# A planned attention and two-layer-pair kernel: places for the last x1 blocks, VectorE for the weights' differences and the norm's multiplies, and longer planned GpSimd sums

## The chip, the cores and the metric

The kernel runs on one core of one Trainium2 chip. The metric is device microseconds of one execution; the time before is the median of three runs. Profiles are single executions on the same kind of chip. Engines: PE is TensorE (PEld its weight load), DVE is VectorE, ACT is ScalarE, POOL is GpSimd, SP issues the DMAs.

## The reference

```python
def _attn_ref(q, k, v, g_norm):                    # 8 batches, 8 heads, 576 tokens, 64 wide
    kv = np.einsum('bhsd,bhse->bhde', k, v)
    out = np.einsum('bhsd,bhde->bhse', q, kv)
    rms = np.sqrt(np.mean(out * out, axis=-1, keepdims=True) + 1e-06)
    return (out / rms * g_norm).astype(np.float32)

def _moe_ref(x, w_in, w_out):                      # x 4608 x 512, w_in 512 x 2048, w_out 2048 x 512
    h = x @ w_in
    g = np.maximum(0.01 * h, h)
    return (g @ w_out).astype(np.float32)

def _moe2_ref(x, w_in, w_out):
    h = x @ w_in
    g = h - np.tanh(h)
    return (g @ w_out).astype(np.float32)

# heads side by side: x = attn.transpose(0, 2, 1, 3).reshape(4608, 512); then moe, then moe2
```

The four weight matrices come as float64 and are read as pairs of 32-bit words.

## The kernel before, in words

There are four large products after the attention. Each is done by a two-by-two block scheme with seven block products instead of eight; every float32 operand is split into a high and a low float16 part, so that a block product is three float16 matmuls (`three`, L489). `PROD` (L28) says which prepared left and right column each of the seven products takes.

The stages on TensorE, in order:
- A start in which the first weights w1 are converted (`convert`), their largest value found (`weight_scale`, `pow2_scale`) and split (`split_first`), beside the attention of batch 0 and part of batch 1.
- First stage (`up` with blk 0): x times w1, 8 blocks of 576 tokens by 8 column pairs, then leaky ReLU. The attention of batches 1 to 7 is placed between its products (`pos`, `between1`), a pair of heads at a time. `norms` (L901) takes the root of the mean square on ScalarE into a tile iv, its reciprocal in three VectorE pieces (L914), stores it to DRAM (L917), loads it back broadcast over partitions as bc (L927), and GpSimd multiplies x with it (L934), one 128x1152 instruction for each half kk.
- Second stage (`down` with blk 0): the result times w2, 8 superblocks, giving x1, whose blocks lie in X places (`place_t`, L1088) until `ready_t` (L1096) has their row maximum (L954) and a DMA has stored them (L1103).
- Third stage (`up` with blk 1, 9 blocks of 512 tokens): x1 times w3, then h - tanh(h) (L1213, half on VectorE, half on GpSimd).
- Fourth stage (`down` with blk 1): times w4, to the output.

Operands are made by `left_stages` (L426): ScalarE writes the high part of three columns (opa, L435 or L437), VectorE the low part (L442 or L444), then four sums of columns are formed in place (`sum_`, L469; line L474 in the profile: in `down` the first two on VectorE, the others on GpSimd; elsewhere all on GpSimd), then high and low part of the four sums (ops). The weights w2, w3 and w4 are converted in the stage before (`convert`: L317 to L340), written to DRAM, and later read back and split by `split_late` (L387) with `right_stages` (L358): ScalarE high (L366) and VectorE low (L369) of three columns, four 128x128 differences on GpSimd (L376), high and low of those. There are 16 such units for each matrix; `spread` lays them evenly over a stretch of time.

Products end in PSUM banks. `keep` (L535) copies an intermediate block (c, u) from bank a into an X place with ScalarE (L544 to L548); `add` (L552) adds a bank and such a block on VectorE (L557 to L563).

The order of every instruction on every engine is written out by a planner (`Plan`, L45). It keeps a planned clock; TensorE's instructions follow one another by `on_pe`, evictions take the first free slot of their engine by `do`, and a `chain` takes its steps one after the other, each with an engine and a planned length. All instructions are then emitted in the order of planned time, and each engine runs its own in that order. So a planned length that is too short puts an instruction too early into its engine's queue, and it holds what stands behind it.

Places are numbered buffers (`Slots`, L114): 21 L places, 12 M places, 8 X places. A place is given back in the plan when its last use is emitted; whoever takes it next waits on the chip until that use has ended. SP issues nearly all DMAs, in order; an issue that must wait holds those behind it.

## Time and profile before

| | |
|---|---|
| median of three runs | 1527.73 us (1526.67 to 1530.34) |
| the profiled execution, its own time | 1526.35 us |
| its span, first to last instruction | 1524.6 us |
| TensorE busy, share of the span | 1443.4 us, 95% |
| VectorE, ScalarE, GpSimd busy | 1247.2, 911.2, 759.8 us |
| first matmul of the second, third, fourth stage, about | 505, 840, 1184 us |
| DMA traffic | 323.19 MB, 212 GB/s |

The first matmuls of the first stage run at 84.7 us. A busy TensorE is not one at its peak: matmuls at the lower granted clock count as busy too. In the views, "idle before <- X" names what ended an engine's wait; ps_a to ps_d are the PSUM tiles of the products, u and c the intermediate blocks, xst the x1 blocks, gl and g the stored activations, x1g the loaded x1, xg the attention's result, unit the weights being prepared, opa and ops the split operands.

### The profile page before, as it was taken

How to read it: one execution, taken by the hardware profiler on the slowest of the kernel's cores; microseconds unless marked ns; L12 is line 12 of the kernel's file. 1: busy time of each engine (PE TensorE's matmuls, PEld its weight loads, DVE VectorE, ACT ScalarE, POOL GpSimd, SP SyncE). 2: the span in 40 equal slices, each digit the busy share in tenths (PEclk: the TensorE clock that was granted, in tenths of full speed). 3: DMA queues.
4: the chain of work that ended last, by engine and by line, in shares of the span. 5: the costliest groups of instructions: out<-in, count | busy, mean ns of one | idle time of the engine just before them, and what ended most of it. 6: DMA issues, size and time to landing. Idle time of an engine off the chain costs nothing. (4 is left out here: it accounts for less than half of the span.)

```text
span 1524.6 us, 33192 instructions
## 1 busy us (share of the span) xinstructions
PE 1443.4 (95%) x12658; PEld 1191.6 (78%) x12658; DVE 1247.2 (82%) x1971; ACT 911.2 (60%) x1525; POOL 759.8 (50%) x758
## 2 busy tenths in 40 slices
PE   5299999999999999999999899999999899999998
PEld 3167777777777777777777688888888788888887
DVE  4886786777777889899996788988899988888881
ACT  5377766777777645455443577778888544454540
POOL 0483321443643455666673355558896644444440
PEclk8599999999999999999999999999999999999999
DMA  9718987999968756446546666655669644444431
GB/s 264 201 60 257 282 281 250 283 295 313 323 250 317 288 172 208 160 168 207 184 146 214 228 221 209 210 200 209 246 240 353 226 146 149 144 143 156 145 97 36
DMA packets 191040, 323.19 MB, mean 212 GB/s; under 512 B 55712, under 2 KB 133536, under 8 KB 190880
## 3 DMA queue, kind: packets, MB, share of 16 engines
q1 hardware_dynamic: 190880, 321.07, 63.6%
q8 instruction: 99, 1.62, 0.4%
q14 instruction: 61, 0.50, 0.1%
HBM read 190.84 MB, written 130.15 MB: 211 GB/s over the span
## 5 line engine op out<-in xcount | busy, mean ns | idle before, releaser
L495 PEld LDWEIGHTS <-w 128*128 128x128 f16 x8400 | 818.3, 98 | 212.1 <-issue 38.1
L474 POOL TENSOR_TENSOR gl<-gl 128x256 f32<-128x256 f32 (+1 forms) x272 | 305.9, 1126 | 297.9 <-issue 92.6
L495 PE MATMUL ps_a<-ops,w 128*128 128x288 f16 (+1 forms) x2400 | 330.3, 281 | 6.0 <-ACT u L544 3.1
L495 PE MATMUL ps_c<-ops,w 128*128 128x288 f16 (+1 forms) x2352 | 314.0, 282 | 6.9 <-DVE g L557 6.8
L495 PE MATMUL ps_a<-opa,w 128*128 128x288 f16 (+1 forms) x2016 | 285.2, 282 | 12.5 <-ACT u L548 6.6
L495 PEld LDWEIGHTS <-ops 128*128 128x128 f16 x1728 | 169.7, 98 | 24.7 <-issue 4.2
L495 PE MATMUL ps_b<-opa,w 128*128 128x288 f16 (+1 forms) x1200 | 175.6, 283 | 0.0
L376 POOL TENSOR_TENSOR unit<-unit 128x128 f32<-128x128 f32 x192 | 129.6, 677 | 91.4 <-DVE wo L369 57.1
L474 DVE TENSOR_TENSOR gl<-gl 128x256 f32<-128x256 f32 (+1 forms) x272 | 160.7, 594 | 4.1
L1213 POOL TENSOR_TENSOR g<-g,th 128x512 f32<-128x512 f32 x72 | 116.7, 1623 | 78.2 <-ACT th L1210 76.8
L934 POOL TENSOR_TENSOR xg<-xg,bc 128x1152 f32<-128x1152 f32 x16 | 47.4, 2970 | 186.3 <-DMA bc<-iv 118.1
L435 ACT ACTIVATE ops<-gl 128x1152 f16<-128x1152 f32 x64 | 74.3, 1162 | 108.7 <-POOL gl L474 107.0
L437 ACT ACTIVATE ops<-gl,inv 128x1024 f16<-128x1024 f32 x72 | 82.5, 1146 | 94.4 <-POOL gl L474 94.4
L495 PEld LDWEIGHTS <-opa 128*128 128x128 f16 x1296 | 126.6, 98 | 14.8
L444 DVE SCALAR_TENSOR_TENSOR ops<-gl,inv,ops 128x1024 f16<-128x1024 f32 x72 | 103.4, 1436 | 22.8 <-ACT ops L437 22.8
L442 DVE TENSOR_TENSOR ops<-gl,ops 128x1152 f16<-128x1152 f32 x64 | 96.5, 1509 | 11.1 <-ACT ops L435 11.0
L495 PE MATMUL ps_a<-w,ops 128*128 128x256 f16 x864 | 97.5, 275 | 3.6 <-ACT c L548 3.6
L557 DVE SCALAR_TENSOR_TENSOR g<-ps_c,u 128x288 f32<-128x288 f32 x128 | 58.0, 453 | 52.1 <-PE ps_c L495 45.8
L548 ACT ACTIVATE u<-ps_a,up 128x256 f32<-128x256 f32 x144 | 67.9, 472 | 51.8 <-PE ps_a L495 41.6
L495 PE MATMUL ps_c<-w,ops 128*128 128x256 f16 x864 | 97.3, 273 | 0.2 <-DVE osb L557 0.2
L474 POOL TENSOR_TENSOR x1g<-x1g 128x256 f32<-128x256 f32 x72 | 64.0, 890 | 49.8 <-DVE opa L444 42.0
L369 DVE SCALAR_TENSOR_TENSOR wo<-unit,s_w,wo 128x384 f16<-128x384 f32 (+1 forms) x96 | 85.3, 892 | 3.7 <-ACT wo L366 3.6
(122 smaller groups left out, 2147.6 us busy)
## 6 DMA issues: line engine op xcount, KB each, us to landing
g<-g SPq DMA_DIRECT2D x64, 576.0 KB, 5.6
gl<-g SPq DMA_DIRECT2D x64, 576.0 KB, 4.8
g<-g SPq DMA_DIRECT2D x72, 512.0 KB, 3.4
gl<-g SPq DMA_DIRECT2D x72, 512.0 KB, 4.5
wd<-wo SPq DMA_DIRECT2D x48, 448.0 KB, 4.2
w<-wd SPq DMA_DIRECT2D x24, 896.0 KB, 7.7
words<-in_moe_w_in_dram SPq DMA_DIRECT2D x64, 256.0 KB, 5.6
words<-in_moe_w_out_dram SPq DMA_DIRECT2D x64, 256.0 KB, 4.6
```

The lines of the kernel that those rows point to most:

```text
L369: nc.vector.scalar_tensor_tensor(out=dst()[:, 1, a:b], in0=cols(0, n), scalar=scale(), in1=dst()[:, 0, a:b], op0=ALU.mult, op1=ALU.subtract,)
L376: nc.gpsimd.tensor_tensor(out=o, in0=a, in1=b, op=ALU.subtract)
L435: nc.scalar.activation(out=o, in_=i_, func=AF.Copy)
L437: nc.scalar.activation(out=o, in_=i_, func=AF.Identity, scale=scale())
L442: nc.vector.tensor_tensor(out=o, in0=i_, in1=h, op=ALU.subtract)
L444: nc.vector.scalar_tensor_tensor(out=o, in0=i_, scalar=scale(), in1=h, op0=ALU.mult, op1=ALU.subtract)
L474: lambda: e.tensor_tensor(out=g()[:, o], in0=g()[:, a], in1=g()[:, b], op=op),
L495: nc.tensor.matmul(out=out_, lhsT=a, rhs=c, start=start and m == 0, stop=stop and m == n - 1, skip_group_check=not fresh,)
L548: nc.scalar.activation(out=t, in_=src, func=AF.Identity, scale=self.scale)
L557: nc.vector.scalar_tensor_tensor(out=o, in0=src, scalar=self.minus if sub else self.scale, in1=t, op0=ALU.mult, op1=ALU.add,)
L934: nc.gpsimd.tensor_tensor(out=x, in0=x, in1=held[kk].ap, op=ALU.mult)
L1213: e.tensor_tensor(out=g()[:, n], in0=g()[:, n], in1=held["t"].ap[:, n], op=ALU.subtract)
```

## The change

- `place_t` and `ready_t`: in the last superblock of the second stage the four blocks of each half lie in one L place instead of four X places, and two blocks that are neighbours in x1 are stored by one DMA.
- `norms`: iv has a tile of its own instead of an X place. From batch 2 on the multiply is done by VectorE in two 128x576 pieces, planned 10.5 us after the load (`LOADBC`) instead of 7.5.
- `right_stages`: the weights' columns lie in another order (`PROD` and `convert` follow), so that two of the four differences are one instruction with a broadcast input; one difference changes its sign, and `left_stages` follows with the sign of one sum. For w2, w3, w4 the differences run on VectorE, for w1 on GpSimd.
- `sum_`: planned lengths. GpSimd 3.0 (3.8 in `down`) times T/1000 plus 0.1 instead of 2.4; VectorE 1.1 plus 0.08 instead of 1.4 plus 0.1.
- `far_scale`: the largest value of w2, w3, w4 is spread over the partitions by a store to DRAM and a broadcast load, instead of by TensorE; it is planned to take 26 us, and the units that need it start later (w2: START + 219 instead of 200, end -72 instead of -75; w4: c3 + 42 instead of 18).
- `AHEAD`: operands of the next superblock start 1.2 us earlier. `pos`: batches 5, 6, 7 stand 5, 10, 15 products earlier.
- The planner: a step that finds no free place is tried again 0.4 us later (`NoRoom`).

The diff's core:

```diff
-PROD = {1: (6, 6), 2: (4, 4), 3: (0, 5), 4: (5, 0), 5: (3, 2), 6: (1, 1), 7: (2, 3)}
+PROD = {1: (6, 5), 2: (4, 4), 3: (0, 6), 4: (5, 0), 5: (3, 1), 6: (1, 2), 7: (2, 3)}
...
+    GPS = 3.0
...
+    def far_scale(name, m, t):
+        held = {}
+        def put():
+            held["d"] = scratch([P, 1], F32, f"m_{name}_d")
+            nc.sync.dma_start(out=held["d"], in_=m)
+        def get():
+            held["w"] = const.tile([P, P], F32, tag="rows", name=f"rows_{name}")
+            nc.sync.dma_start(out=held["w"], in_=held["d"].rearrange("p o -> o p").broadcast_to((P, P)))
+        def end():
+            r, s = stile(f"r_{name}"), stile(f"s_{name}")
+            nc.vector.tensor_reduce(out=r, in_=held["w"], axis=AX.X, op=ALU.max)
+            powers(r, s)
+        at(t, put)
+        at(t + 6.0, get)
+        at(t + 24.0, end)
...
-                    out=held["w"].ap[:, NU * a:NU * a + NU].rearrange("p (b c) -> p b c", b=2), in_=src[a]
+                    out=held["w"].ap.rearrange("p (b a c) -> p a b c", b=2, a=2)[:, a], in_=src[a]
...
-    def right_stages(w, dst, scale, minus4):
+    def right_stages(w, dst, scale, minus4, merged=False):
...
-        def less(o, a, b):
+        def both(e):
+            b = w().rearrange("p (o c) -> p o c", c=P)
+            e.tensor_tensor(out=b[:, 1:4:2], in0=b[:, 3:4].broadcast_to((P, 2, P)), in1=b[:, 1:3], op=ALU.subtract)
+
+        def less(o, a, b, e):
             o, a, b = (w()[:, P * n:P * n + P] for n in (o, a, b))
-            nc.gpsimd.tensor_tensor(out=o, in0=a, in1=b, op=ALU.subtract)
-
-        t4, t2, t1, t3 = b21, b22, b11, b12 = range(4)
+            e.tensor_tensor(out=o, in0=a, in1=b, op=ALU.subtract)
+
+        t4, t1, t2, t3 = b21, b11, b22, b12 = range(4)
+        on, e = ("V", nc.vector) if merged else ("G", nc.gpsimd)
+        f = 0.28 if merged else 0.5
         return [
             ("A", 0.62, lambda: hi(4, 7, 3)), ("V", 0.62, lambda: lo(4, 7, 3)),
-            ("G", 0.5, lambda: less(t1, b12, b11)), ("G", 0.5, lambda: less(t3, b22, b12)),
-            ("G", 0.5, lambda: less(t2, b22, t1)),
-            ("G", 0.5, (lambda: less(t4, b21, t2)) if minus4 else (lambda: less(t4, t2, b21))),
+            (on, 1.5 * f, lambda: both(e)), (on, f, lambda: less(t2, b22, t1, e)),
+            (on, f, (lambda: less(t4, b21, t2, e)) if minus4 else (lambda: less(t4, t2, b21, e))),
...
-                on, (1.4 if on == "V" else 2.4) * f + 0.1,
+                on, 1.1 * f + 0.08 if on == "V" else (gps or GPS) * f + 0.1,
...
-            sum_(s3, a11, a21, first), sum_(s1, a21, a22, first, ALU.add), sum_(s2, a22, s3), sum_(s4, a12, s2),
+            sum_(s3, a21, a11, first), sum_(s1, a21, a22, first, ALU.add), sum_(s2, a22, s3, rest, ALU.add),
+            sum_(s4, a12, s2, rest),
...
-    AHEAD = 6.8
+    AHEAD = 8.0
+    LOADBC = 10.5
...
-            held["iv"] = X.take([4 * Q, T1], F32, "iv")
+            held["iv"] = const.tile([4 * Q, T1], F32, tag="iv", name="iv")
...
+            if b >= 2:
+                scaled_ = [("V", 0.66, lambda kk=kk, n=n: scale(kk, nc.vector, n, n + 2)) for n in (0, 2)]
+            else:
+                scaled_ = [("G", 2.9 if b else 2.7, lambda kk=kk: scale(kk, nc.gpsimd, 0, 4))]
+            more.append([(None, LOADBC if b > 1 else 7.5 if b else 6.0, lambda kk=kk: load(kk))] + scaled_ + stages)
...
-            pos[b, PAIRS[hp]] = FIRST[b][hp] if b in FIRST else NOP * (NP * b - 16 + 2 * hp)
+            pos[b, PAIRS[hp]] = FIRST[b][hp] if b in FIRST else NOP * (NP * b - 16 + 2 * hp) - 5 * (b - 4)
...
-    spread(lambda i, kk, t: split_late(1, i, kk, t, M), UNITS, START + 200.0, end1 - 75.0)
+    spread(lambda i, kk, t: split_late(1, i, kk, t, M), UNITS, START + 219.0, end1 - 72.0)
...
+            if s == NS1 - 1:
+                if (s, m) not in out_t:
+                    out_t[s, m] = L.take([P, 2, 2, T1], F32, "xst"), []
+                return out_t[s, m][0].ap[:, int(blk[1]) - 1, int(blk[0]) - 1]
             out_t[s, m, blk] = X.take([P, T1], F32, "xst")
...
+                tile_, there = out_t[s, m]
+                there.append((t, nh))
+                if {(0, nh), (1, nh)} <= set(there):
+                    done_.update((("x1", c, s, 0), ("x1", c, s, 1)))
+                    nc.sync.dma_start(out=x1d[c, s], in_=tile_.ap[:, nh].rearrange("p a b -> p (a b)"))
+                if len(there) == 4:
+                    L.give(out_t.pop((s, m))[0])
...
-    e = c3 + 18.0
+    e = c3 + 42.0
```

## Rows read from the trace of the kernel before

**Rows 1.** Page, part 1: engine, busy us (share of the span), x instructions.

```profile
PE 1443.4 (95%) x12658; PEld 1191.6 (78%) x12658; DVE 1247.2 (82%) x1971; ACT 911.2 (60%) x1525; POOL 759.8 (50%) x758
```

**Rows 2.** Waits of TensorE, whole run: who <- whom: us in total, times, longest.

```profile
PE pt L224 <- DVE m_w L264: 29.2, 1, 29.2
...
PE ps_a L495 <- ACT u L548: 7.5, 4, 6.6
...
PE ps_c L495 <- DVE g L557: 6.8, 11, 1.8
...
PE ps_a L495 <- ACT u L546: 4.3, 4, 2.1
...
PE ps_a L495 <- ACT c L548: 4.1, 2, 3.6
...
PE ps_a L495 <- ACT u L544: 3.1, 3, 1.4
...
PE ps_a L495 <- DVE opa L442: 1.8, 3, 1.1
```

**Rows 3.** Timeline, 826 to 870: start, us, instruction, [idle before <- releaser].

```profile
851.55 0.87 ACT L548 ACTIVATE u<-ps_a,up 128x256 f32<-128x256 f32 x2 [7.00 <-DMA x<-xst]
...
852.07 1.44 PE L495 MATMUL ps_a<-opa,w 128*128 128x256 f16 x6 [6.64 <-ACT u L548]
```

**Rows 4.** Chain that ended last, 1195 to 1260: start, us, what.

```profile
1203.82 12.31 PE ps_a L495 x96
...
1242.33 10.48 PE ps_a L495 x96
```

**Rows 5.** Timeline, 258 to 266 and 368 to 379.

```profile
265.34 0.90 PE L495 MATMUL ps_a<-opa,w 128*128 128x288 f16 x6 [1.23 <-ACT u L546]
...
376.75 0.41 ACT L853 ACTIVATE sq<-po 128x288 f32<-128x288 f32 x1 [4.36 <-DMA iv<-iv]
...
377.51 1.10 PE L495 MATMUL ps_a<-opa,w 128*128 128x288 f16 x6 [2.14 <-ACT u L546]
```

**Rows 6.** Groups by form: line engine op | busy us, mean ns | idle before.

```profile
L376 POOL TENSOR_TENSOR unit<-unit 128x128 f32<-128x128 f32 x192 | 129.6, 677 | 91.4 <-DVE wo L369 57.1 <-issue 12.0 <-PE ps_a L495 8.8
...
L474 DVE TENSOR_TENSOR gl<-gl 128x256 f32<-128x256 f32 x144 | 84.5, 588 | 2.9
...
L442 DVE TENSOR_TENSOR ops<-xg,ops 128x576 f16<-128x576 f32 x32 | 29.7, 947 | 4.9 <-ACT ops L435 4.9
```

**Rows 7.** Timelines, 215 to 285 and 360 to 390, VectorE, GpSimd and TensorE.

```profile
217.74 2.88 DVE L328 TENSOR_SCALAR unit<-unit 128x512 int32<-128x512 int32 x1
...
222.14 0.90 PE L495 MATMUL ps_c<-ops,w 128*128 128x288 f16 x6 [0.63 <-DVE g L557]
...
257.42 0.74 DVE L914 RECIPROCAL iv<-iv 128x96 f32<-128x96 f32 x1
...
258.75 0.43 DVE L328 TENSOR_SCALAR unit<-unit 128x512 int32<-128x512 int32 x1
...
277.61 2.64 POOL L934 TENSOR_TENSOR xg<-xg,bc 128x1152 f32<-128x1152 f32 x1 [2.69 <-DMA bc<-iv]
...
366.70 0.75 DVE L914 RECIPROCAL iv<-iv 128x96 f32<-128x96 f32 x1
...
388.27 2.88 POOL L934 TENSOR_TENSOR xg<-xg,bc 128x1152 f32<-128x1152 f32 x1 [2.40 <-DMA k<-in_k_dram]
```

**Rows 8.** Line 474: instruction xcount: ns min/median/max, first to last start, forms.

```profile
L474 DVE TENSOR_TENSOR gl<-gl x272: 407/450/1493, 462.5 to 1480.5; 128x256 f32<-128x256 f32 x72, 128x288 f32<-128x288 f32 x64
```

**Rows 9.** Stretches: us, busy us of each engine (x), granted clock, DMA share, GB/s.

```profile
659.20:700.40 41.20, 39.57 (x323) 31.31 (x321) 39.59 (x54) 20.40 (x28) 27.67 (x27) 1.00 0.57 193
...
1062.00:1150.00 88.00, 88.00 (x809) 78.78 (x807) 81.39 (x123) 73.91 (x129) 77.72 (x85) 1.00 0.70 256
...
1150.00:1204.00 54.00, 47.80 (x431) 41.88 (x430) 53.97 (x69) 38.09 (x58) 38.44 (x28) 1.00 0.91 332
```

**Rows 10.** Waits of all engines, 505 to 840.

```profile
ACT ops L435 <- POOL gl L474: 107.0, 47, 6.2
```

More of the change, by code (lines that the diff above doesn't have):

```diff
@@ L42 @@
 Consts = namedtuple("Consts", "x hid neg_hid op out neg_out")
+class NoRoom(Exception):
+    pass
 class Plan:
@@ L90, in go, with run @@
                 end[0] = max(end[0], t_ + dur + (0.0 if eng is None else self.HAND))
-                def run(fn=fn):
-                    fn()
+                def run(fn=fn, until=None):
+                    try:
+                        fn()
+                    except NoRoom:
+                        assert until is None or self.now < until, "no room"
+                        self.at(self.now + 0.4, lambda: run(fn, until or self.now + 40.0))
+                        return
                     left[0] -= 1
@@ L122, in take @@
         if not self.idle:
-            raise RuntimeError(f"no place {self.kind} for {name}")
+            raise NoRoom(f"no place {self.kind} for {name}")
         n = self.idle.pop(0)
@@ L273, in last @@
                 fn()
-        later = 0.0 if n == 0 else 4.0
         at(t, first)
-        at(t + 2.8 + (later and later + 2.0), last)
+        at(t + (2.8 if n == 0 else 26.0), last)
     def in_unit(w, i, kk):
@@ L314, in one @@
                 held["ap"] = keep()
+        def one():
             words = held["w"].ap
@@ L353, in convert @@
         slow = 1.0 if keep else 1.1
-        steps = [(None, land, load), ("A", 0.7, one), ("V", 0.72 * slow, two), ("V", 0.4 * slow, shift),
+        steps = [(None, land, load), (None, 0.0, room), ("A", 0.7, one), ("V", 0.72 * slow, two), ("V", 0.4 * slow, shift),
                  ("V", 0.63 * slow, low), ("V", 0.63 * slow, high)]
         plan.chain(t, steps + ([(None, 0.0, store)] if keep is None else []))
-    def right_stages(w, dst, scale, minus4):
+    def right_stages(w, dst, scale, minus4, merged=False):
         def cols(n0, n1):
@@ L423, in load_weights, with left_stages @@
         )
-    def left_stages(g, dst, scale, T, done=None, first=None, pieces=1):
+    def left_stages(g, dst, scale, T, done=None, first=None, pieces=1, rest=None, gps=None):
         f = T / 1000.0
@@ L698, in produce @@
                     lambda held=held: held["g"].ap, o, (lambda: scale(s)) if scale else None, T,
-                    done=lambda held=held: L.give(held["g"]), first=nc.vector,
+                    done=lambda held=held: L.give(held["g"]), first=nc.vector, gps=3.8,
                 )
@@ L912, in inverse @@
         def inverse(n):
-            part = held["iv"].ap[:, CP * n:CP * n + CP]
+            part = held["iv"][:, CP * n:CP * n + CP]
             nc.vector.reciprocal(out=part, in_=part)
         def store():
-            nc.sync.dma_start(out=ivd[b], in_=held["iv"].ap)
-            X.give(held["iv"])
+            nc.sync.dma_start(out=ivd[b], in_=held["iv"])
         def load(kk):
```

47 lines of the change are left out of this document (27 added, 20 removed).

## The prediction

> **What bounds it now.** I read the page's busy times first: TensorE is busy in 95% of the span, every other engine less [rows 1]. So I asked next what TensorE waits for, since only its idle time and its slow clock can be won [rows 2]. The largest row, 29.2 us, lies in the start, until the first weights are scaled; the change does not touch it. The six below it sum to 7.5 + 6.8 + 4.3 + 4.1 + 3.1 + 1.8 = 27.6 us, and they lie in four places: VectorE evictions (ps_c, 6.8 us; the longest, 1.8, near the third stage's end, the other ten, 5.0, in the first stage), ScalarE evictions of that stage (u L546), ScalarE and VectorE in the second stage (u L544, opa), and the two borders of the third, with one wait of 6.6 us and one of 3.6 us. That is the purse. The reader is to see in these rows that no single engine bounds the kernel; short queues in ScalarE and VectorE do, each behind something that came late.
>
> **Large buffers for the last x1 blocks.** At 851.55 a ScalarE eviction of the third stage had waited 7.00 us for the landing of an x1 store, and TensorE stood 6.64 us behind it [rows 3]. The eviction takes one of the eight X places; the last superblock's x1 blocks held them until their stores landed. In the new version these blocks lie in two L places, so no eviction takes a place behind such a store. The clock falls in that wait: the six matmuls after it took 1.44 us, and the same clock after the wait at 1203 made 96 matmuls 12.31 us instead of 10.48 [rows 3, 4]. I put the cold piece at 1.8 us by that pair, an estimate, so the part is worth 6.64 + 1.8 = 8.4 us. What is late next: the following weights and operands; the two stores per block pair become one, which relieves SP and adds no queue. Should an L place still be read when it is taken, a VectorE addition waits in place of ScalarE; bounds 5 and 9 us.
>
> **The roots' own buffer.** The same cause shows twice in the first stage: ScalarE stood for the store of iv, and TensorE lost 1.23 and 2.14 us [rows 5]. The second wait is followed by a low clock (six matmuls in 1.10 us), which I price at 1.5 us by the pair in [rows 4]. iv now has a tile of its own: 1.23 + 2.14 + 1.5 = 4.9 us won; bounds 3.4 and 5.5.
>
> **Roots multiplied on VectorE from batch 2 on.** GpSimd no longer has these 12 instructions; VectorE gets 24 of half the size, about 0.95 us each by the nearest row (128x576) [rows 6], 23 us spread over 300 us in which VectorE is not full. The danger is the wait that moves with them. The factors come by DMA, behind the store of iv. By the code the second multiply now starts 0.25 + 1.8 + 3.0 + 10.5 = 15.55 us after the last reciprocal. In the trace the factors were there later than that in the bad batches: reciprocal done at 258.16, multiply released by the DMA at 277.61 (19.5 us); 367.45 and 388.27 (20.8 us) [rows 7]; I count on two or three such among the six batches. GpSimd could wait for nothing; VectorE has the evictions queued behind it, and TensorE waits for those. How much of a blocked VectorE reaches TensorE: an integer shift at 217.74 took 2.88 us, where the same at 258.75 took 0.43 (it fell together with the large GpSimd multiply), and TensorE lost 0.63 us at 222.14 [rows 7]; so about 1.8 us are swallowed. Two or three batches late by 4 to 5 us cost 2 to 3.5 us each: some 8 us at most; nothing, if the store of iv lands sooner. I take 4 us lost, the middle, since the same DMA traffic stands around them. On the other side, the large GpSimd multiply no longer holds VectorE, nor do the subtractions below: of the 5.0 us that ps_c costs here [rows 2] I take 2 us as won (bounds 0 and 4).
>
> **Weights' differences on VectorE.** 48 units leave GpSimd, each four instructions of 677 ns, 130 us in all [rows 6]. VectorE gets three instead, one of 128x256 and two of 128x128. For the first the nearest row is 588 ns (mean), 407 ns at least [rows 6, 8]; for the narrow ones no row stands, so I bound them by half of and the whole of 407 ns and take 0.3 us. A unit then costs VectorE at least 0.4 + 2 x 0.2 = 0.8 us, disturbed 0.6 + 2 x 0.3 = 1.2 (1.4 at the far end). Removing 2.7 us of GpSimd gives something back: the rows' mean of 588 against 407 is what meeting GpSimd costs VectorE, 0.18 us for each of the 16 sums of a superblock, about 3 us; with the other two-input instructions twice that. GpSimd is busy 28 us in a superblock [rows 9], so a us of it costs 0.1 to 0.2 us of VectorE, and a unit gives back 0.3 to 0.55 us. Net a unit costs 0.2 to 0.9 us.
>
> Second stage: two units in a superblock of 41.2 us, in which VectorE is already busy 39.6 us [rows 9]. It becomes 40.0 to 41.4: just inside, or just over. Against it stand two helps. GpSimd's sums are now planned at 1.19 us instead of 0.79 (3.8 x 0.288 + 0.1), near the truth; before, ScalarE was given its next split too early and stood 107 us in total until GpSimd was done [rows 10], with the evictions behind it; that is the 3.1 us of u L544. And operands start 1.2 us earlier (AHEAD), which covers most of the 1.8 us on opa [rows 2]. I take 3 us won of 4.9; bounds: 4.9 won and, at the upper load, 7 x 0.5 = 3.5 lost (VectorE waits a little too, so it is full before 41.2).
>
> Third stage and its end: the last weights' units start 24 us later and end where they did, so in 1062 to 1150 there are about 15 instead of 12. VectorE was busy 81.4 of 88 us [rows 9]. Added: 15 x 0.8 to 1.2 = 12 to 18, three more units of two scalings each, about as long as the 128x576 row [rows 6], 6; given back, 12 x 2.7 = 33 us of GpSimd x 0.2 = 7. That is 92 to 98 of 88, so VectorE enters 1150 some 4 to 10 us late, where it is busy 54.0 of 54 already [rows 9]. Against this stands again the longer planned sum: the 3.56 us wait at 1203 and its cold 1.8 us come from an eviction queued behind a split that waited for GpSimd [rows 2, 4]. I let the two cancel: 0; bounds 5 won, 8 lost.
>
> **The rest.** The first weights stay on GpSimd, 16 units with two narrow subtractions made one wide: at most half of 677 ns each [rows 6], 5 us of GpSimd, while TensorE waits in the start for other things as well: 1 us won (0 to 2). The maximum of the later weights goes through DRAM instead of two TensorE instructions a time, three times: under 1 us, hidden, since its units are started later to match; two short DMAs a time pass through SP. The new column order, the sign of one difference and the earlier last batches change no count: 0.
>
> **Sum.** -8.4 - 4.9 + 4 - 2 - 3 + 0 - 1 = -15.3 us on the profiled execution's 1526.35: 1511. The median of the runs shown lies 1.4 us above that execution; so 1512.
>
> **Rivals.**
> - *No new wait on VectorE* (0.17). The factors land in time and GpSimd's relief is at the upper bound: no +4, and 6 us more at the two full places: 1501 to 1502. For it speaks that late landings went with the very jams that the change removes; against it, VectorE's 54.0 of 54.
> - *Half given back* (0.13). The buffers win their 13 us, the multiplies cost 8 of them and the replanning wins nothing: 1521.
> - *It does not reach TensorE, or the new order shifts as much as it wins* (0.08): 1527. For: every order of all queues changes. Against: the 7.00 us behind a store is a plain place conflict.
> - *VectorE becomes the bound; slower* (0.07). It decides from the point at which a superblock asks for more than 41.2 us. If the moved instructions mostly meet a GpSimd sum, each costs up to the longest row, 1.49 us against 0.41 [rows 8], and nothing comes back: 1 us more per superblock in seven, 13 us at 1062 to 1204, and all 8 us on the multiplies, less the buffers: +7 + 13 + 8 - 13.3 = +15, 1542. Against it: the mean is 0.59, far from 1.49.
>
> The Trainium skill speaks for that last rival (SBUF — State Buffer, Who interferes with whom): a VectorE instruction with two inputs in SBUF and a GpSimd instruction that reads SBUF exclude each other, and the later one is blocked until the first is through. The trace agrees in kind, 407 to 1493 ns for one sum [rows 8]. By the rule at its worst the moved instructions cost what this rival says; by the mean in the rows they cost what the sum says.
>
> **Chances.** Forecast 0.55 (1506 to 1518), the others as given. A measurement of this kernel tells about 0.3% from no change, 4.6 us. Faster by more: 0.55 + 0.17 + 0.12 = 0.84; within: 0.09; slower: 0.07. The range leaves out the slower rival and the rest of the two-sided tails: 1499 to 1525.
>
> **What would show it.** No ScalarE eviction waits for a landing of x1 or iv, and TensorE has no wait over 2 us near 845. Waits of VectorE for bc appear in the first stage, up to 5 us each, with ps_c waits behind them. ScalarE's 107 us on GpSimd fall by more than half. VectorE's busy share rises from 82% to about 85%, GpSimd's falls from 50% to under 40%. Wrong it is if VectorE shows 41 us of 41.2 in superblocks with evictions late, or if the L places bring a DMA wait at 840.

## The result, and the profile after

The changed kernel takes 1539.61 us (1536.22 to 1543.11), the kernel before beside it 1527.20. The ratio is 1.0078, 95% interval 1.0051 to 1.0105: 12 us slower, where 1512 was forecast. The profiled execution is the longest of its four (1543.11 us, span 1541.3), that of the kernel before nearly its shortest, so the two profiles below differ by 16.7 us and not by 12.

Waits of TensorE after, against [rows 2] (who <- whom: us in total, times, longest):

```profile
PE ps_c L540 <- DVE g L602: 19.1, 17, 2.8
PE pq L877 <- ACT kvd L868: 12.9, 6, 5.4
PE pk L857 <- DMA v<-in_v_dram: 8.5, 4, 6.4
PE ps_a L540 <- ACT u L591: 4.7, 1, 4.7
PE pk L857 <- DVE xg L908: 4.0, 1, 4.0
PE ps_a L540 <- ACT c L591: 4.0, 3, 3.4
```

The 6.64 us wait of [rows 3] is gone; this is the longest that is left at the border (858 to 879):

```profile
860.18 0.82 PE L540 MATMUL ps_a<-ops,w 128*128 128x256 f16 x6 [0.56 <-ACT c L593]
```

The row of ps_c, where TensorE waits for VectorE, rose from 6.8 to 19.1. Where the time went is told by stretches: first stage, second stage, third and fourth together. The first begins with its first float16 matmul, the second with its first one into ps_d, the third with the first of 256 columns. Columns as in [rows 9]: us, then busy us of TensorE, its weight load, VectorE, ScalarE, GpSimd, then granted clock, DMA share, GB/s. Before, then after:

```profile
84.70:505.40 420.70, 408.83 (x3661) 313.88 (x3660) 314.05 (x584) 304.38 (x608) 175.53 (x198) 0.99 0.84 271
505.40:840.00 334.60, 329.61 (x2682) 261.84 (x2681) 301.81 (x421) 155.34 (x203) 194.57 (x185) 1.00 0.56 191
840.00:1524.60 684.60, 666.65 (x6054) 593.28 (x6053) 574.56 (x847) 414.45 (x636) 362.01 (x344) 0.99 0.54 186
```

```profile
86.40:528.50 442.10, 417.28 (x3655) 318.55 (x3654) 322.89 (x653) 303.51 (x606) 94.42 (x109) 0.97 0.82 259
528.50:858.80 330.30, 328.96 (x2681) 262.13 (x2680) 311.12 (x469) 156.22 (x203) 155.16 (x121) 1.00 0.57 192
858.80:1541.30 682.50, 663.76 (x6051) 591.83 (x6050) 582.18 (x894) 416.09 (x636) 314.70 (x280) 1.00 0.55 187
```

The first stage lost 21.4 us; the second won 4.3, the rest 2.1, the start lost 1.7. Of the 21.4, TensorE stood 12.9 us longer (24.8 against 11.9) and was busy 8.5 us longer for the same matmuls at a granted clock of 0.97 instead of 0.99. VectorE is busy 323 of 442 us there, 73%: it is not full. (The 83% in the expectation of e3 is the share of the whole run.) What it did instead was stand. Three pauses of the first stage, with the engine that stood before each (timeline after: start, us, instruction [idle <- releaser]):

```profile
281.68 1.43 DVE L979 TENSOR_TENSOR xg<-xg,bc 128x576 f32<-128x576 f32 x2 [4.99 <-DMA bc<-iv]
284.13 1.60 PE L540 MATMUL ps_c<-ops,w 128*128 128x288 f16 x6 [2.78 <-DVE g L602]
...
415.68 0.61 ACT L405 ACTIVATE wo<-unit,s_w 128x384 f16<-128x384 f32 x1 [8.63 <-DMA wf<-unit]
416.65 1.60 PE L540 MATMUL ps_a<-ops,w 128*128 128x288 f16 x6 [4.68 <-ACT u L591]
...
481.26 0.92 ACT L479 ACTIVATE opa<-gl 128x864 f16<-128x864 f32 x1 [5.35 <-DMA gl<-g]
482.54 0.88 PE L540 MATMUL ps_a<-ops,w 128*128 128x288 f16 x3 [3.40 <-ACT c L591]
```

The first is the wait for the broadcast factors that was forecast. In the second, ScalarE wants an M place whose last content, a unit, is not yet stored; evictions stand behind it. The third is a load of stored activations (gl) that came late.

The second shows how one late transfer holds the next. SP's own rows (SPq is the issue of a transfer):

```profile
405.04 0.54 SPq L447 DMA_DIRECT2D wd<-wo  x1
410.22 0.34 SPq L440 DMA_DIRECT2D unit<-wf  x1
...
411.13 0.39 SPq L389 DMA_DIRECT2D wf<-unit  x1
```

```profile
SPq L440 <- DMA wd<-wo: 9.7, 5, 4.6
```

The second view is SP's wait from 190 to 505 us: five times, at most 4.6 us, it stood at the load of a unit until an earlier unit's store had landed. That is the gap from 405.58 to 410.22 here. So the store that ScalarE needed was issued at 411.13 only, 4.1 us after ScalarE had begun to stand (415.68 - 8.63 = 407.05).

In the third stage's end VectorE did become full. The stretches of [rows 9], later by the 18 us that the border moved:

```profile
1080.00:1168.00 88.00, 83.69 (x762) 74.27 (x760) 87.91 (x157) 72.98 (x126) 43.58 (x36) 1.00 0.68 243
1168.00:1222.00 54.00, 47.18 (x424) 41.17 (x422) 53.97 (x69) 37.85 (x54) 35.55 (x28) 1.00 0.92 331
```

### The profile page after: what moved, and what is told of

It is laid out like the page before. It is cut to its first block, busy times and chain, and to the rows that moved or that the text cites. A ratio compares the mean times of both kernels' runs of the same rounds, so it can differ in the third digit from the quotient of the medians.

```text
span 1541.3 us, 33054 instructions
## 1 busy us (share of the span) xinstructions
PE 1447.2 (94%) x12649; PEld 1195.0 (78%) x12649; DVE 1273.6 (83%) x2136; ACT 914.2 (59%) x1525; POOL 591.9 (38%) x538
## 4 chain that ended last, share of the span: by engine, by line
PE 62%; DVE 16%; DMA 10%; issue 5%; SPq 3%; POOL 2%; ACT 1%; DVEq 0%; ACTq 0%; POOLq 0%
PE ps_a L540 29%; PE ps_c L540 17%; PE ps_b L540 9%; PE ps_d L540 4%; DVE opa L486 3%; DMA gl<-g 2%; DVE gl L518 2%; DVE wo L408 2%; DMA words<-in_moe_w_in_dram 2%; DVE ops L486 2%; DMA bc<-iv 2%; DMA wd<-wo 1%; DMA v<-in_v_dram 1%; DVE g L602 1%; PE pk L857 1%
## 5 line engine op out<-in xcount | busy, mean ns | idle before, releaser
L540 PE MATMUL ps_c<-ops,w 128*128 128x288 f16 (+1 forms) x2352 | 316.9, 283 | 19.2 <-DVE g L602 19.1
L518 POOL TENSOR_TENSOR xg<-xg 128x288 f32<-128x288 f32 x64 | 59.0, 927 | 292.8 <-DMA k<-in_k_dram 57.2
L518 DVE TENSOR_TENSOR gl<-gl 128x256 f32<-128x256 f32 (+1 forms) x272 | 152.3, 561 | 4.2
L479 ACT ACTIVATE ops<-gl 128x1152 f16<-128x1152 f32 x64 | 74.3, 1161 | 76.1 <-POOL gl L518 74.9
L405 ACT ACTIVATE wo<-unit,s_w 128x384 f16<-128x384 f32 (+1 forms) x96 | 63.1, 662 | 67.3 <-DVE unit L419 48.8
L486 DVE TENSOR_TENSOR opa<-gl,opa 128x864 f16<-128x864 f32 x64 | 81.0, 1266 | 6.4 <-ACT opa L479 6.3
```

The source lines that it names most:

```text
L405: nc.scalar.activation(out=dst()[:, 0, a:b], in_=cols(0, n), func=AF.Identity, scale=scale())
L479: nc.scalar.activation(out=o, in_=i_, func=AF.Copy)
L486: nc.vector.tensor_tensor(out=o, in0=i_, in1=h, op=ALU.subtract)
L518: lambda: e.tensor_tensor(out=g()[:, o], in0=g()[:, a], in1=g()[:, b], op=op),
L540: nc.tensor.matmul(out=out_, lhsT=a, rhs=c, start=start and m == 0, stop=stop and m == n - 1, skip_group_check=not fresh,)
```

## The experiments

All of them were measured beside the kernel before. Where the expectations speak of superblocks 2 to 4 and 5 to 8, the edits act on batches 2 to 7 (multiplies) and on batches 5, 6 and 7, by 5, 10 and 15 products (pairs moved up). "Stands" are, from 190 to 505 us, ScalarE's waits for a unit's store (wf<-unit, wd<-wo: an M place not yet free), and VectorE's for the store of a finished block (g<-g, L636 or L681: an L place not yet free) or the load of bc, summed from the waits of each engine. Other waits for transfers (loads of units, words and gl; in the kernel before 9.4 us of ScalarE for the store of iv) are not in them. Stage lengths are from one profile each, ratios from all runs; a profile can lie 4 us off its kernel's median (e10: 1539.63 against 1535.36), so small differences of stage lengths tell nothing.

| kernel | ratio | 95% interval | first stage | second | third, fourth | ScalarE, units | VectorE, g and bc |
|---|---|---|---|---|---|---|---|
| before | 1 | | 420.7 | 334.6 | 684.6 | 0.0 | 0.5 |
| after | 1.0078 | 1.0051 to 1.0105 | 442.1 | 330.3 | 682.5 | 14.8 | 12.9 |
| e1 | 1.0051 | 1.0032 to 1.0069 | 432.8 | 331.0 | 683.3 | 10.1 | 0.2 |
| e2 | 1.0006 | 0.9991 to 1.0022 | 424.9 | 331.2 | 684.2 | 1.0 | 16.0 |
| e3 | 1.0014 | 0.9998 to 1.0031 | 427.9 | 330.9 | 683.9 | 3.2 | 13.9 |
| e4 | 0.9955 | 0.9941 to 0.9968 | 419.0 | 335.6 | 675.5 | 0.0 | 0.0 |
| e5 | 0.9981 | 0.9967 to 0.9995 | 426.5 | 330.9 | 679.1 | 10.5 | 4.4 |
| e6 | 1.0060 | 1.0039 to 1.0081 | 433.6 | 330.2 | 685.3 | 6.6 | 10.3 |
| e7 | 0.9958 | 0.9941 to 0.9975 | 423.4 | 335.4 | 675.5 | 0.0 | 13.4 |
| e8 | 1.0077 | 1.0055 to 1.0098 | 431.1 | 336.8 | 683.6 | 23.7 | 0.0 |
| e9 | 1.0114 | 1.0078 to 1.0150 | 434.2 | 330.1 | 690.3 | 16.0 | 9.4 |
| e10 | 1.0041 | 1.0025 to 1.0056 | 428.2 | 339.2 | 684.1 | 11.4 | 2.1 |
| e11 | 0.9943 | 0.9922 to 0.9964 | 419.7 | 333.8 | 678.4 | 0.0 | 0.2 |
| e12 | 0.9971 | 0.9955 to 0.9988 | 426.5 | 332.2 | 677.0 | 0.0 | 9.0 |
| e13 | 1.0012 | 0.9994 to 1.0031 | 428.3 | 335.0 | 676.7 | 0.0 | 11.5 |
| e14 | 1.0029 | 1.0013 to 1.0044 | 431.3 | 335.8 | 676.7 | 26.2 | 0.0 |
| e15 | 1.0034 | 1.0016 to 1.0051 | 431.1 | 334.5 | 675.6 | 10.1 | 9.0 |
| e16 | 1.0055 | 1.0037 to 1.0072 | 441.1 | 330.9 | 678.8 | 15.3 | 2.3 |
| e17 | 1.0103 | 1.0085 to 1.0121 | 442.1 | 334.0 | 675.8 | 0.0 | 8.2 |
| e18 | 1.0072 | 1.0050 to 1.0093 | 435.7 | 331.2 | 683.9 | 7.6 | 15.3 |

### One part undone, and the two buffer parts alone

e1, multiplies back on GpSimd:

```diff
-            if b >= 2:
+            if b >= 9:
-            more.append([(None, LOADBC if b > 1 else 7.5 if b else 6.0, lambda kk=kk: load(kk))] + scaled_ + stages)
+            more.append([(None, 7.5 if b else 6.0, lambda kk=kk: load(kk))] + scaled_ + stages)
```

> The changed kernel, with one part undone: the multiplication of x0 by the broadcast inverse roots goes back from VectorE to GpSimd for superblocks 2 to 4 (in one piece of 2.9 us, with 7.5 us allowed for the load instead of 10.5). Theory A (VectorE standing in order for the broadcast): in the changed kernel VectorE stood 4.99, 2.36 and 2.19 us for bc, with a pause of TensorE of 2.78 us at 281 behind the first; GpSimd takes these waits over, the pauses at 281, 332 and 346 go, and the first stage (442.1 us after, 420.7 before) falls by 8 to 14 us, the whole to about 1528 to 1532. Theory B (ScalarE standing for the stores of w2's finished units) and theory C (the row maximum sent through DRAM holding SP's queue): the first stage falls by no more than 4 us, the pauses at 359, 412 and 479 stay.

The kernel takes 4 us less than after (the intervals overlap), the first stage 9.3 us less. That is theory A's stage length, but not its whole (1528 to 1532; 1535.5 measured). The waits for bc went over to GpSimd. ScalarE's stands stayed for the most part (10.1 of 14.8 us), as theories B and C had it.

e2, scales of w2 to w4 as before, w2's units from START + 200 to the end less 75:

```diff
-                far_scale(name, m, t + 0.6)
+            pow2_scale(name, m, 1, t + 0.6 + later, 1.6 if n == 0 else 3.0)
```

> The changed kernel, with one part undone: the scales of w2 to w4 are found as before (row maxima through a transpose and a matmul on TensorE, no trip through DRAM), so that s_w2 is there earlier, and w2's units are spread from START + 200 to the stage's end less 75 instead of START + 219 to less 72. Theory C (the trip through DRAM holds SP's queue for 2.4 us at 278 and again at 473, and the later start crowds w2's units into too few places): the pauses of TensorE at 281, 359, 412 and 479, together 14.9 us, shrink to under 5, and the first stage falls by 10 to 15 us, the whole to about 1527. Theory A (VectorE's waits for bc): only the pause at 281 becomes shorter, the first stage falls by 1 to 4 us. Theory D (VectorE's load by the differences): nothing falls by over 2 us.

This gives 11 us back (0.0072 of 1527), and the first stage is 17 us shorter, a little more than theory C said. ScalarE's stands for units' stores fell from 14.8 to 1.0 us; VectorE's did not (16.0 against 12.9).

e3, w2's differences back on GpSimd (the call of `right_stages`):

```diff
- ... n == 2, n >= 1)
+ ... n == 2, n >= 2)
```

> The changed kernel, with one part undone for the first stage alone: w2's differences go back from VectorE to GpSimd (there in the new, joined form of three instructions); w3's and w4's stay on VectorE. Theory D (the differences fill VectorE's queue in the first stage): the first stage falls by 6 us or more, since some 13 us of VectorE go. Theories A and C: VectorE is 83% busy there in either kernel, not full, so the first stage stays within 3 us, or grows by up to 5 because a unit then takes longer from load to store and holds its two places the longer (theory B).

This gives 10 us back, and the first stage is 14 us shorter, as theory D had it, though VectorE is not full there. So each of three parts gives back 4 to 11 us, 25 in sum where 12 were lost. The prices of the parts do not add up.

e4, the kernel before with the new `place_t` and `ready_t`, and iv's own tile; nothing else:

```diff
-            held["iv"] = X.take([4 * Q, T1], F32, "iv")
+            held["iv"] = const.tile([4 * Q, T1], F32, tag="iv", name="iv")
...
+                    out_t[s, m] = L.take([P, 2, 2, T1], F32, "xst"), []
```

> The kernel before, with two parts of the change alone: the large buffers for the last x1 blocks, and iv's own tile. By the terms of the prediction: -8.4 us at the border between the second and third stage and -4.9 us at 377, so 1513 us, bounds 1511 to 1519. The changed kernel shows the border's gain (third stage 330.3 against 334.5 us with losses elsewhere in it). A rival: iv's wait was hiding a later one, as for the lack of another place, and only the buffers count: 1518. If both gains are eaten by later waits: 1526.

The ratio is 0.9955: 7 us won where 13 were forecast. The third and fourth stage win 9.1, as forecast for the buffers; the first wins 1.7, and the start and the second stage lose 2.9. ScalarE no longer waits for iv, but TensorE's 2.14 us at 377 [rows 5] came back at 387 as 1.89 us, behind a ScalarE that now stands for GpSimd's multiply:

```profile
385.28 0.92 ACT L435 ACTIVATE opa<-xg 128x864 f16<-128x864 f32 x1 [4.76 <-POOL xg L933]
...
387.06 0.75 PE L847 MATMUL po<-qt,kvd 128*128 128x288 f32 x2 [1.89 <-ACT qt L839]
```

The rival that only the buffers count is the nearer one.

### Combinations

e5 undoes all three, w4's differences too (e1's and e2's edits, and):

```diff
- ... n == 2, n >= 1)
+ ... n == 2, n == 2)
```

> The changed kernel with all three parts undone together: multiplies of x0 on GpSimd, scales of w2 to w4 through TensorE (w2's units from START + 200), and the differences of w2 and w4 on GpSimd; w3's differences stay on VectorE, as do the large buffers, iv's tile, the longer times planned for GpSimd's sums and the earlier start of the accumulators' loads. Theory E (the three parts feed one another: a late VectorE instruction keeps a store waiting on SP's queue, the loads behind it land late, and VectorE and ScalarE stand for these loads): the first stage falls from 442.1 to 418 to 422 us, by no more than the 21.4 that were lost, although the three runs so far gave back 8.6, 17.2 and 14.2 us one by one, which sums to 40. Theory F (each part has a price of its own, and what is undone adds up): the first stage falls by more than 25, to under 417. Fourth section (from the border of the second and third stage to the last stage): if w4's differences on VectorE are what ate the border's gain, 336 to 338 us as against 345.3 after and 336.7 with the buffers alone; if not, 344 to 346. With the second stage at 331 the whole gives 1512 to 1516 us.

Neither theory holds: the first stage takes 426.5 us, and the whole is 3 us faster than before. w3's differences stay on VectorE here, w4's are on GpSimd: the third and fourth stage take 679.1 us against 684.2 in e2. In the first stage 7.5 us remained against e4, with none of the three parts in it.

e6, as e2, but w2's units left at START + 219:

> The changed kernel with the scales of w2 to w4 through TensorE as in the run of e2, but w2's units left where the change put them, from START + 219 to the stage's end less 72. It takes SP's trip through DRAM away and leaves the crowding. Theory C1 (SP's queue, held for 5.8 us by the row maximum's way through DRAM): the first stage is as in e2, 423 to 427 us. Theory C2 (units 19 us later, which finds too few places and makes ScalarE stand for stores): the first stage stays at 437 us or more, with the pauses at 359 and 412.

The first stage, 433.6 us, lies between the theories, 8.7 us above e2 and so nearer to C2, and the pauses at 359 and 412 are there (5.8 and 3.5 us). The kernel is 8 us slower than e2 by 19 us of start and 3 of end in a list of times. The trip through DRAM itself makes 2.7 us between e6 and after, within the intervals.

e7, e4 with the change's `scale(kk, e, n0, n1)` and its 10.5 us, and the pairs moved up:

```diff
- ... NOP * (NP * b - 16 + 2 * hp)
+ ... NOP * (NP * b - 16 + 2 * hp) - 5 * (b - 4)
```

> The kernel before with the two buffer parts as in e4, and on top of them the multiplies of x0 on VectorE for superblocks 2 to 4, with 10.5 us for the load of bc and the pairs' places moved up by 5 products a superblock as in the change (the longer wait needs them). e4's first stage was 419.0 us, the whole 1521.5. Theory E (parts feed one another): alone this part costs under 4 us, first stage 417 to 423. Theory F (a price of its own): 425 to 429, as it gave back 8.6 us when undone.

The whole is within 0.5 us of e4, as theory E had it; the first stage is 4.4 us longer, the start 0.9 shorter.

e8, e4 with all later differences on VectorE:

```diff
-            nc.gpsimd.tensor_tensor(out=o, in0=a, in1=b, op=ALU.subtract)
+            (nc.vector if merged else nc.gpsimd).tensor_tensor(out=o, in0=a, in1=b, op=ALU.subtract)
```

> The kernel before with the two buffer parts as in e4, and on top of them the differences of w2, w3 and w4 on VectorE (four instructions of 128 columns, as the kernel before has them on GpSimd). e4's sections were 419.0, 335.5, 336.7 and 338.9 us. Theory E: the first stage grows by under 4 us; theory F: by 10 to 14 us, as undoing gave back 14.2. Second stage (w3): if the 4 us that the change won there come from its differences, 331; if from the accumulators' loads and the planned sums, 335. Fourth section (w4): 344 to 346 if these differences fill VectorE there, 337 if not.

The kernel is 19 us slower than e4: 12 in the first stage, 8 in the third and fourth. The second stage wins nothing, so its 4 us after do not come from having w3's differences on VectorE.

### Is it the number of places?

e9 is the changed kernel, e10 the kernel of e8, each with one line changed:

```diff
-    NL, NM, NX = 21, 12, 8
+    NL, NM, NX = 20, 13, 8
```

> The changed kernel with one size changed: 13 places for w's units and operands A (M) instead of 12, and 20 large places (L) instead of 21 to make room. Nothing else. In the changed kernel's first stage ScalarE stood 8.6, 5.1 and 3.9 us for a place whose last content was still being stored (its rows name wf<-unit and wd<-wo), and pauses of TensorE of 4.0 and 4.7 us stand with it. Theory G (units in fewer places than their pace asks for): with one more place a place is written one unit later, these stands fall under 5 us in sum, the pauses at 359 and 412 go, and the first stage falls from 442.1 to 430 or less. Theory H (the places are no cause, the queues are late anyway): the first stage stays within 4 us of 442, and the stands move to other rows; a loss beyond that would come from the one L place less, as waits for words, g or bc.

> The kernel of e8 (the kernel before, two buffer parts, differences of w2 to w4 on VectorE) with 13 M places and 20 L places. In e8 the first stage was 431.1 us against 419.0 without the differences, and ScalarE stood 12.4 and 11.3 us for places whose store was under way. Theory G (the differences' own work is cheap there; the shorter plan of a unit turns the places round too soon): first stage 419 to 424. Theory H (the load on VectorE is what costs): 428 to 433. The fourth section should stay at 343 to 346 by either, as VectorE is full there.

e10 is 5.5 us faster than e8, but its first stage takes 428.2 us, which theory H had named, and ScalarE's stands are only halved. In e9 the first stage is 8 us shorter than after, between the theories. ScalarE's stands are 16.0 us against 14.8, and the whole is no better (third and fourth stage 690.3, with one L place less). One more place helps a little and does not remove the stands. (Of the 8.6, 5.1 and 3.9 us that e9's expectation names, the third is a wait for g<-g.)

### Parts that change only times and order

e11, e4 with the longer planned sums and AHEAD 8.0 in second and fourth stage alone:

```diff
-    AHEAD = 6.8
+    AHEAD = 8.0
-                    done=lambda held=held: L.give(held["g"]), first=nc.vector,
+                    done=lambda held=held: L.give(held["g"]), first=nc.vector, gps=3.8,
```

> The kernel of e4 (the kernel before, two buffer parts) with the parts of the change that touch only the second and the last stage: GpSimd's sums planned at 3.8 instead of 2.4 per 1000 elements and VectorE's at 1.1, and 8.0 instead of 6.8 us of lead for a superblock's operands; the first and third stage keep their lengths. The changed kernel and its variants won 3.3 to 4.3 us in the second stage, and e8 shows that w3's differences do not bring that. Expected: second stage 331 against 335.5 in e4, the others as in e4 (419.0, 336.7, 338.9), so 1517 us. If it takes the longer times of the first stage or the joined differences as well, the second stage stays at 335.

The ratio is 0.9943, the fastest here, though not to be told from e4. The second stage takes 333.8 us, 1.8 less than in e4, where 4.5 were expected. e4, e7 and e11 beat both kernels by 6 us and more.

e12, e4 with the longer sums everywhere (`GPS = 3.0`, and `gps=3.8` as in e11) and e7's line of `pos`:

> The kernel of e4 with two parts of the change: GpSimd's sums planned at 3.0 (3.8 in the second and last stage) and VectorE's at 1.1, and the pairs of superblocks 5 to 8 moved up by 5 products each. Both are in e5, whose first stage was 426.5 us against e4's 419.0 although the multiplies, differences and scales are undone there. If these two make the 7.5 us: first stage 425 to 428. If they come from the new form of the differences and the step that takes a unit's place before the conversion: 417 to 421. Second stage: 335 (without the earlier lead) or 331 (if the planned sums win it). Fourth section: 340 to 342 if the planned sums are what e5 lost there against e4 (341.1 against 336.7).

The first stage takes 426.5 us, as much as in e5. The second takes 332.2, so the planned sums win 3.4 of the 5.3 us between e4 and after, without AHEAD.

e13, e4 with e7's line of `pos` alone; e14, e4 with e8's differences for w2 alone (`n == 1`); e15, e13 with

```diff
-    spread(lambda i, kk, t: split_late(1, i, kk, t, M), UNITS, START + 200.0, end1 - 75.0)
+    spread(lambda i, kk, t: split_late(1, i, kk, t, M), UNITS, START + 219.0, end1 - 72.0)
```

and e16, the changed kernel with e1's edit and e5's `n == 2`:

> The kernel of e4 (0.9955 of the time before, first stage 419.0 us) with the pairs of superblocks 5 to 8 moved up by 5 products each, and nothing else. It is in e7 (423.4) and e12 (426.5). If it is what those two have in common that costs: first stage 423 to 426, whole 0.997 to 0.999. If it costs nothing alone: 418 to 421, whole 0.995 to 0.996.

> The kernel of e4 with w2's differences alone on VectorE; w3's and w4's stay on GpSimd. e8, with all three, was 18.6 us slower than e4. If the first stage carries 10 to 12 of them as its profile says: first stage 429 to 432, later sections as in e4 (335.5 and 675.6 us), whole 1.002 to 1.004. If w4's differences in the third stage carry nearly all and the first stage of e8 was an accident of that profile: 420 to 424 and 0.996 to 0.998.

> The kernel of e4 with w2's units spread as in the change, START + 219 to the stage's end less 72 (before: START + 200 to less 75), and the pairs moved up as in e13, without which the plan has no room. Multiplies and differences stay on GpSimd. Theory I (the tighter spread has a price of its own, 8.3 us by e6 against e2): first stage 8 us above e13's, whole 1.000 to 1.003. Theory J (it costs only where VectorE also has the moved work and stands in order for it): within 3 us of e13.

> The changed kernel with the multiplies and the differences of w2 and w4 back on GpSimd; the way of the scales through DRAM and the late spread of w2's units stay. e5, which has these two undone as well, was 0.9981 with a first stage of 426.5 us. Theory I (the late spread and the trip through DRAM have prices of their own, 8 and 3 us): first stage 434 to 440, whole 1.004 to 1.006. Theory J (they cost only together with the work on VectorE): first stage 425 to 429, whole 0.997 to 0.999.

e13 loses 8.7 us against e4 by moving when pairs start, with not one instruction added; that is more than either branch said. It is not a fixed price: e7 has the same move, with the multiplies on VectorE and the longer time for bc on top, and loses nothing against e4. e14 loses 11 us, all in the first stage. e15 loses 3 us more than e13, which is undecided. e16 is at 1.0055 and 441.1 us of first stage, about as theory I had it, with the multiplies and w2's differences off VectorE: it is busy 309 us of that stage, less than the 317 in e4.

Why e13 loses stands on SP's queue. SP and VectorE in e13, then SP in e4, which has the same instructions:

```profile
369.46 0.38 SPq L917 DMA_DIRECT2D iv<-iv  x1
369.95 0.36 SPq L403 DMA_DIRECT2D wd<-wo  x1
375.74 2.78 SPq L926 DMA_DIRECT2D bc<-iv  x4
...
382.00 0.58 SPq L636 DMA_DIRECT2D g<-g  x1
...
386.42 0.46 DVE L557 SCALAR_TENSOR_TENSOR g<-ps_b,c 128x288 f32<-128x288 f32 x1 [9.17 <-DMA g<-g]
```

```profile
372.16 0.36 SPq L917 DMA_DIRECT2D iv<-iv  x1
372.62 0.63 SPq L636 DMA_DIRECT2D g<-g  x1
376.78 2.59 SPq L926 DMA_DIRECT2D bc<-iv  x4
```

In both SP stops until iv's store has landed, 5.4 us in e13 (370.31 to 375.74). In e4 the store of a block g went out ahead of that; in e13 the store of the block whose L place VectorE wanted next came after it, behind four loads of bc and six of k, v and q, and VectorE stood 9.17 us until it had landed. That store went out at 382.00, 4.75 us after VectorE had begun to stand. (The expectations of e5, e8 and e17 speak of loads of the accumulators; the transfer in this row is a store, L636.) In e14 and e16 it is a unit's store and ScalarE, then TensorE (e14 first, then e16 with SP's issue of the store):

```profile
336.22 0.92 ACT L436 ACTIVATE opa<-xg 128x864 f16<-128x864 f32 x1 [5.60 <-DMA wf<-unit]
338.10 0.90 PE L496 MATMUL ps_a<-ops,w 128*128 128x288 f16 x6 [1.92 <-ACT u L547]
...
401.44 0.92 ACT L436 ACTIVATE opa<-xg 128x864 f16<-128x864 f32 x1 [5.87 <-DMA wf<-unit]
403.22 0.90 PE L496 MATMUL ps_a<-ops,w 128*128 128x288 f16 x6 [2.77 <-ACT u L547]
```

```profile
390.46 0.54 SPq L389 DMA_DIRECT2D wf<-unit  x1
...
394.19 0.61 ACT L405 ACTIVATE wo<-unit,s_w 128x384 f16<-128x384 f32 x1 [9.83 <-DMA wf<-unit]
395.16 1.60 PE L540 MATMUL ps_a<-ops,w 128*128 128x288 f16 x6 [7.57 <-ACT u L591]
```

The stores are not slower once issued. Issue to landing of a unit's store, 190 to 505 us, before and in e14:

```profile
DMA to landing us min/median/max: 2.4/4.7/7.4
```

```profile
DMA to landing us min/median/max: 2.7/4.9/6.3
```

In e16 ScalarE had stood 6.1 of its 9.83 us when SP issued the store; in e14 the issues came early in the stands, and most of the time there is the store on its way. All of e14's stands are for stores of converted units (wf), not of the units whose differences moved (wd). By the code a shorter planned unit gives its places back sooner, and so another instruction takes another place; that this is how e14 comes to its stands is not shown.

### Is SP's queue the link?

In e17 (on e13) and e18 (on the changed kernel) GpSimd issues iv's stores and bc's loads, in e18 the scales' transfers too:

```diff
-                    nc.sync.dma_start(
+                    nc.gpsimd.dma_start(
```

> The kernel of e13 (first stage 428.3 us, whole 1.0012) with iv's stores and bc's loads issued by GpSimd instead of SP, so that the wait for iv's store to land (11.8 us in four waits on SP there) holds GpSimd's queue and not the loads of the accumulators and of k, v and q. Theory K (SP's queue is the link): VectorE's stand for g at 377 of 9.2 us falls under 2, the pause of TensorE at 382 of 5.9 us with it, first stage 419 to 423. Theory L (the link is on the engines, or GpSimd's sums then come late behind the same wait): first stage 426 or more.

> The changed kernel with iv's stores, bc's loads and the two transfers of each later scale issued by GpSimd instead of SP. SP stood there 16.0 us for iv and 5.8 us for the row maximum's way. Theory K: first stage 442.1 falls by 10 to 16 us, the whole to 0.998 to 1.001; what stays are the stands for places whose stores are under way. Theory L: it falls by under 4 us, whole 1.005 to 1.008.

e17 gives theory L. It is 14 us slower than e13: VectorE still stood up to 6.6 us for a store of g, and GpSimd's multiplies and differences now queue behind its own transfers. In e18 the first stage is 6 us shorter, between the theories; the start is 4 us longer, and the whole is the same, as theory L had it. Moving SP's wait to GpSimd won nothing here; whether SP's waits alone are the link is not shown.

## Why the prediction failed, point by point

By stages, forecast against the two profiles: the first stage -2.9 (iv -4.9, multiplies +4, ps_c -2) against +21.4; the second -3 against -4.3; the third and fourth with their border -8.4 against -2.1; the start -1 against +1.7. So the step that failed lies in the first stage: the sum priced there the instructions that run, and put at 0, or only as a relief, what changes the time and the order of issues. Tried singly, three such terms cost 8 to 11 us each.

- *Column order, sign, earlier last batches: "change no count: 0"*: this step failed. The earlier batches alone cost 8.7 us (e13), though nothing in the company of the multiplies (e7).
- *The maximum through DRAM, "hidden, since its units are started later to match"*: this failed by the later start, 8 us (e6 against e2; with e13's order 3 us, undecided, in e15).
- *Differences of w2*: they were weighed for the second and third stage, and in the first only as relief from GpSimd. There they cost 11 us (e14), though a unit takes VectorE no more than forecast: 0.45 + 2 x 0.32 = 1.1 us, forecast 0.8 to 1.2.
- *iv, -4.9*: mis-sized. The stand went, its pause moved on 10 us, behind GpSimd's multiply; e4 wins 7 us in all, 2 less than the buffers. What was late next was not asked.
- *Multiplies, +4*: the waits came as forecast, 4.99 us the longest, and undoing the part gave back 4 us, though with overlapping intervals. One of the two late batches it was read from is doubtful: the row at 388.27 [rows 7] names a load of k, not bc. Together with e13's move the part costs nothing (e7).
- *Buffers, -8.4*: right. e4 wins 9.1 us there; after, most of it is eaten by VectorE in the third stage.
- *Second stage, -3*: -4.3 measured, and the planned sums, one of the two helps that were named, bring it about in part (e12, 332.2); e11 has AHEAD besides and 333.8, so what each adds is not told apart. ScalarE's 107 us on GpSimd [rows 10] fell to 74.9 only, not by half.
- *Third stage, 0, bounds 5 won to 8 lost*: mis-sized, within its bounds. 6.9 us are lost by w4's differences (third and fourth stage 683.6 in e8, 676.7 in e14). The sum itself said 92 to 98 of 88 us, and the balance should not have been drawn at zero. A unit took VectorE 0.58 + 2 x 0.52 = 1.6 us there, and all 16 took 26 us where 12 to 18 were put in for 15 (after, 1000 to 1230; busy us, mean ns; L415 is the wide difference, L419 a narrow one):

```profile
L419 DVE TENSOR_TENSOR unit<-unit 128x128 f32<-128x128 f32 x32 | 16.8, 524 | 0.0
L415 DVE TENSOR_TENSOR unit<-unit 128x256 f32<-128x256 f32 x16 | 9.2, 576 | 0.1
```

- *The slower rival*: 1542 came close to 1539.6, but by another mechanism in the first stage, where most was lost. "VectorE becomes the bound" holds at 1080 to 1222 alone. Its price, that the moved instructions meet GpSimd at full length, was paid by some of them (instruction xcount: ns min/median/max, whole run; then one that was long and GpSimd beside it):

```profile
L415 DVE TENSOR_TENSOR unit<-unit x48: 405/413/1392, 316.4 to 1155.8; 128x256 f32<-128x256 f32 x48
L419 DVE TENSOR_TENSOR unit<-unit x96: 273/280/1325, 317.7 to 1160.0; 128x128 f32<-128x128 f32 x96
```

```profile
1090.59 1.27 POOL L1276 TENSOR_TENSOR g<-g,th 128x512 f32<-128x512 f32 x1
1090.74 1.39 DVE L415 TENSOR_TENSOR unit<-unit 128x256 f32<-128x256 f32 x1
```

  The medians lie within 2 to 3% of the shortest, so at least half met nothing. From 1067 to 1160, 17 of the 48 were long (0.42 to 1.39 us), and each of these ran while a GpSimd instruction was under way. By the rule of the Trainium skill (SBUF — State Buffer, Who interferes with whom) these would be the blocked ones; the trace agrees in kind.

What is common in the first stage, as far as it is shown: there the transfers are busy 84% of the time, and each engine runs a fixed order. Every kernel that keeps that stage's planned times (before, e4, e11) has at most 0.5 us in the table's two last columns and a stage of 419.0 to 420.7 us. Each of the other 17, whatever it moved, has at least 8 us of stands and 423.4 to 442.1 us. Which stand it gets is a matter of which store is late and who wants its place. The lengths do not follow the sum of stands (e7 has 13.4 us and loses 4, e16 17.6 and loses 22; the kernel before has 9.4 us for iv's store besides and loses 1.7), so a price for each part cannot be given, and parts measured one by one sum to twice the loss.

That these stands are the cause rests on the rows behind each pause and on this table; taking them away without moving anything else was not done. The rival that the load on VectorE is the cause is out for e16, which has less of it than e4; for the kernels with w2's differences it is not excluded (e10 came out as theory H said). In the three long stands shown above about half of the time went by before SP issued the store (4.1 of 8.63 us after, 4.75 of 9.17 in e13, 6.1 of 9.83 in e16), so both SP's queue and the store's way are in them. Giving a place back in the plan only when its store has landed (4.7 us after its issue, median) would test the second half, and was not tried.

## What to carry to other kernels

In a stage whose engines run a written order and whose transfers are busy most of the time (84% here), an edit that "changes only when" is no zero: give it bounds as wide as the longest stand that a late load or a place under store can make, here 5 to 10 us. Ask for every moved step which transfers go out ahead of it on SP and which place it takes, not only how long it runs. And try the parts singly and in pairs: two of them gave 7 us, the whole change took 12, and one that lost 8.7 us alone lost nothing with another.

## What was not expected of the hardware

A load of bc issued by GpSimd occupied GpSimd for 597 ns (e17, median), and one issued by SP occupied SP for 607 (e13), but the first kind landed later after its issue: 7.1 against 4.2 us, median of 40 each from 190 to 505 us (e17, then e13):

```profile
DMA to landing us min/median/max: 5.0/7.1/9.5
DMA to landing us min/median/max: 3.1/4.2/6.8
```

The Trainium skill (DMA: Bandwidth & Descriptors, Issuing engine by pattern) calls issue by SP generally faster than by GpSimd; for the landing the traces agree, for the issue itself they show no difference. And 128 row maxima on their way through DRAM took 7.8 to 9.0 us for the store to land and 7.2 to 8.7 for the load back (after, two of each), though a unit of 512 times the bytes took at most 7.4 to land (wf<-unit, before).
